# Attention and a softplus layer on one core: the last queries' shift copied on ACT instead of DVE, and one low part moved to GpSimd

## The chip, the cores and the metric

The kernel runs on one core of a Trainium2 chip. The metric is the device time of one execution in microseconds; lower is better. The time of a kernel is the median of its runs, and one more execution is profiled. TensorE (PE, with its weight loads PEld), VectorE (DVE), ScalarE (ACT), GpSimd (POOL) and SyncE (SP, here only a DMA queue) each run their own list of instructions in order, and wait for one another by semaphores.

## The reference, cut to what matters

Rotary attention over 4 batches of 8 heads, 576 positions of 64 numbers, and a layer of 2304 tokens, 512 to 2048 to 512 wide, with softplus between:

```python
q_rot, k_rot = rotate(q), rotate(k)
scores = q_rot @ k_rot.T / sqrt(64)
attn = exp(scores - max(scores))
attn = attn / (sum(attn) + 1e-9)
x = (attn @ v)          # 2304 tokens of 512
h = x @ w_in
g = max(h, 0) + log1p(exp(-abs(h)))
out = g @ w_out
```

All is float32. The kernel splits every operand in a rounded high part and the low part that is left, and adds three products of parts (high times high, low times high, high times low).

## The kernel before, in words

**Stages.** Attention comes first (to about 342 us of the trace), the layer after it. The heads go two at a time: 16 pairs, each in 9 slots, so 144 slots in all. A pair's 64-wide heads stand on partitions 0 to 63 and 64 to 127, so most products are two matmuls of 64 rows.

**What a slot does.** In slot `s` the first pass `p1(s)` (L448, L455) multiplies queries by keys and DVE takes the row maxima (L457). Ten slots later the second pass `p2` (L503) computes the same scores with keys on the partitions, into one of two buffers of PSUM (tile `sp`, pool `ps_2`), and adds the shift (minus the maximum of each query) by two more matmuls of ones with `sm`, which holds the shift as a row. Then `exps` does two exponentials on ACT: L508 writes the rounded one, `ph`; L511 writes the full one back over `sp`. DVE subtracts (L517, `low`) and gives `pl`. Three slots later `pv_half` (L553) multiplies `ph` and `pl` by the values.

**The shift.** POOL splits the maxima into `sh` (L353, L356, `shift1`). `shift2` turns them from columns into rows by small matmuls with an identity (L475), into the unused columns of the very `sp` buffer that `p2` fills next. Queries come in 4 chunks of 128 and a last one of 64. The chunks go in two groups: group 0 (chunks 0 to 2) in the slot with `r == 0`, group 1 (chunk 3 and the last 64 queries, one copy for each head) in the slot with `r == 4`, where `r` is the slot's number within its pair. `shift3` copies the rows to `sm`, on ACT, between the two exponentials of that tile (L484). The last 64 queries alone are copied by DVE, by two instructions of 64x64 at the end of `shift2` (L479), ahead of the second pass of that tile in the program. The tile after it (`r == 4` of its pair, last keys and all queries) is the first to need group 1, in its last two matmuls, those with `onesd`.

**The ropes.** POOL rotates the pairs ahead of time: multiplies with the tables, adds, rounds (`hl` are queries, `kk` keys; part 1 of each is the low part). Pairs 0 and 1 are split between engines to start sooner; pair 1 is `rope_second`, a generator whose steps the table `ROPES` deals out to the first slots. Its last step is the low part of the queries, on DVE. The first pass of pair 1 (slot 9) needs it in its third matmul. `split_v` rounds the values of a pair on ACT and subtracts on POOL (tile `vs`); a dictionary by slot says how many of its steps a slot takes for pair 0.

**What sets the order.** Instructions that go through `pin` stand on their engine in the order in which the program is written; the DMAs of the loop are chained likewise. Nearly all of the work here is pinned, so the slots' order of calls is the order on the engines. A matmul that writes a buffer waits for every earlier reader of that buffer that stands ahead of it in the program.

Of the kernel before, what the change touches and what calls it, by code (L numbers as in the profile page):

```python
# [8 lines left out]
F32 = mybir.dt.float32  # L9
# [5 lines left out]
ALU = mybir.AluOpType  # L15
# [5 lines left out]
HS = 288  # L21
# [24 lines left out]
    127: (3, 2), 131: (3, 3), 136: (4, 0), 140: (4, 1)}  # L46
SPLITS = {}
LEAD = 3
ROPES = {0: ((1, 4),), 1: ((1, 1),), 2: ((1, 1),), 7: ((1, 1),), 8: ((1, 1), (2, 1)),
         **{s: ((2, 1),) for s in range(9, 18)}}  # L50
FIRST = {8: 0, 9: 1, 10: 2, 11: 3}


# [1 line left out]
def rope_attention_softplus_moe(  # L55
# [8 lines left out]
    nc = tc.nc  # L64
# [19 lines left out]
    pin = tc.keep_in_program_order  # L84
# [221 lines left out]
    def attention(es, es_r, es_s, tail, window):  # L306
# [18 lines left out]
        sm = [at1.tile([128, 5, 128], F32R, name=f"sm{i}") for i in range(2)]  # L325
# [4 lines left out]
        rows = (slice(0, 64), slice(64, 128))  # L330
# [17 lines left out]
        def rnd(out, in_, e):  # L348
            if e == "A":
                pin(nc.scalar.copy(out=out, in_=in_))  # L350
            else:
                e = nc.vector if e == "V" else nc.gpsimd
                pin(e.tensor_scalar(out=out, in0=in_, scalar1=1.0, scalar2=0.0, op0=ALU.mult, op1=ALU.add))  # L353

        def tt(out, in0, in1, op, e):
            pin((nc.vector if e == "V" else nc.gpsimd).tensor_tensor(out=out, in0=in0, in1=in1, op=op))  # L356

        def new_hl(p, i):
            if i:
                hl_t[p, i] = kk[p % 3]  # L360
            else:
                hl_t[p, i] = hl_p.tile([128, 2, S], F32R, tag="hl", name="hl")
            return hl_t[p, i]

        def rope_second():
            (qb, qa), (kb, ka) = [[raw_t[1, i][:, j] for j in range(2)] for i in range(2)]
            q, k = new_hl(1, 0), new_hl(1, 1)
            yield tt(ka, ka, tab[:, 0, :], ALU.mult, "P")
            yield tt(kb, kb, tab[:, 1, :], ALU.mult, "P")
            tt(ka, ka, kb, ALU.add, "P")  # L370
            yield rnd(k[:, 0], ka, "A")
            yield tt(qa, qa, tab[:, 0, :], ALU.mult, "P")
            yield tt(k[:, 1], ka, k[:, 0].bitcast(F32), ALU.subtract, "P")
            yield tt(qb, qb, tab[:, 1, :], ALU.mult, "P")
            tt(qa, qa, qb, ALU.add, "V")
            yield rnd(q[:, 0], qa, "A")
            yield tt(q[:, 1], qa, q[:, 0].bitcast(F32), ALU.subtract, "V")

        def rope_steps(p, e="P"):
            for i in (1, 0):  # L380
# [31 lines left out]
        def load_v(p):  # L412
            chain(nc.sync.dma_start(out=vf[p % 2], in_=v[2 * p:2 * p + 2].rearrange("h p c d -> p h c d")))
# [58 lines left out]
        def shift2(p, g, t):  # L472
            for n, c in enumerate((3, 4) if g else range(3)):
                for i, o in enumerate(rows):
                    pin(nc.tensor.matmul(out=t[:, i, HS + n * 64:HS + n * 64 + 64], lhsT=sh[p % 2][o, c, :],  # L475
                                         rhs=identr[o, o], start=True, stop=True))
            if g:
                for i, o in enumerate(rows):
                    pin(nc.vector.tensor_copy(out=sm[p % 2][o, 4, :64], in_=t[o, i, HS + 64:HS + 128]))  # L479
            return t[:, :, HS:HS + (64 if g else 192)]  # L480

        def shift3(p, g, x):
            cs = slice(3, 4) if g else slice(0, 3)
            pin(nc.scalar.copy(out=sm[p % 2][:, cs, :].rearrange("p c (t x) -> p t c x", t=2),  # L484
                               in_=x.rearrange("p t (c x) -> p t c x", x=64)))

        def tile2(n):
            ps2[n] = ps_2.tile([128, 2, 512], F32, tag="s2", name="sp2")
# [70 lines left out]
        def evac(w):  # L559
            p, j = divmod(w, 2)  # L560
            pv = pv_t.pop(w)
            xt = xt_p.tile([D + 1, 2, HS], F32, tag="xt", name="xt")
            if w >= 2 * NP - 3:
                pin(nc.vector.tensor_copy(out=xt, in_=pv[0:D + 1, :, :HS]))
            else:
                pin(nc.scalar.copy(out=xt, in_=pv[0:D + 1, :, :HS]))
            if w > 2 * NP - 3:
                store(w, xt, free)
            else:
                done.append((w, xt))  # L570
# [71 lines left out]
        def first(s):  # L642
            n = FIRST[s]
            tile2(n)
            p2(n)
            exps(n)

        for s in range(NSLOT + LAG + PVD + 1):
            n2, n3 = s - LAG, s - LAG - PVD
            p, r = divmod(s, PER)  # L650
            has2, has3 = 0 <= n2 < NSLOT, 0 <= n3 < NSLOT
            m = n3 % PER
            for n, part in halves[0].get(n3, ()):
                pv_half(n, part)
            if n3 > 0 and m == 0 or has3 and m == 4:
                evac(2 * (n3 // PER) - (m == 0))
            if s > LAG + 3 and has2:
                tile2(n2)
                g = {0: 0, 4: 1}.get(r) if s <= NSLOT + 4 else None
                x = None if g is None else shift2(p - 1, g, ps2[n2])  # L660
                p2(n2)
                if r == 5 and s < NSLOT:
                    p1(s)
                exps(n2, None if g is None else (lambda: shift3(p - 1, g, x)))
            elif s == LAG - 1:
                first(s)
            elif s == LAG + 3:
                shift3(0, 1, shift2(0, 1, ps_2.tile([128, 2, 512], F32, tag="s2", name="st")))
            for n, part in halves[1].get(n3, ()):
                pv_half(n, part)  # L670
            if s < NSLOT and (r != 5 or not p):
                p1(s)
                if r in (6 - (p == 0), 8):
                    shift0(p, r // 8)
            if s == 0:
                wp = ps_2.tile([128, 2, 512], F32, tag="s2", name="wp")
            if s == LAG - 1:
                wp = ps_v.tile([128, 2, 512], F32, tag="pv", name="wp")
            if s < LAG + PVD - 1 and s != LAG - 2:
                for i, o in enumerate(2 * rows):  # L680
                    pin(nc.tensor.matmul(out=wp[:, i % 2, :HS], lhsT=ones[o, :], rhs=hl_t[0, 0][o, 0, :HS], start=True,
                                         stop=True))
            if s == LAG - 3:
                shift3(0, 0, shift2(0, 0, ps_2.tile([128, 2, 512], F32, tag="s2", name="st")))
            if s != LAG - 1 and s in FIRST:
                first(s)
            for n, part in halves[2].get(n3, ()):
                pv_half(n, part)
            if s in FIRST or s > LAG + 3 and has2:
                low(FIRST.get(s, n2))  # L690
            if s == 6:
                shift1(0, 0)
            if r == 7 and PER < s < NSLOT:
                shift1(p, 0)
            if r == 0 and 0 < s <= NSLOT:
                shift1(p - 1, 1)
            if s < NSLOT:
                for x, z in ROPES.get(s, ()):
                    for _ in range(z):
                        next(ropes[x], None)  # L700
                if r == 7 and 2 < p + 2 < NP:
                    ropes[p + 2] = rope_steps(p + 2)
                x = (s + 2) // PER + 1
                if 2 < x < NP:
                    for _ in range(1 + (r == 5)):
                        next(ropes[x], None)
                if r in (3, 5) and 2 < p + 2 < NP:
                    load(p + 2, int(r == 3), chain)
                if r == 6 and p + 1 < NP:
                    load_v(p + 1)  # L710
                if p and r == 6:
                    sv = split_v(p)
                if p and r == 1:
                    corner(p, 0, chain)
                if s == 4 or p and r == 8:
                    corner(p, 1, chain)
            for _ in range({6: 2, 7: 1, 8: 1}.get(s, int(s > 10 and r in (1, 6, 7, 8)))):
                next(sv, None)
            if done and m in (1, 5):
                store(*done.pop(), chain)  # L720
            if n3 % (PER * NH // 2) == 4 and n3 > 4:
                load_sums(n3 // (PER * NH // 2) - 1, chain)
            if n3 % (PER * NH // 2) == 7 and n3 > 7:
                guard(n3 // (PER * NH // 2) - 1)
            if n3 % (PER * NH // 2) == 9 and n3 > 9:
                recip(n3 // (PER * NH // 2) - 1)
            tail(s)
            window(s)
# [151 lines left out]
```

## Time and profile before

| | before |
|---|---|
| median of 3 runs | 749.22 us (748.53 to 750.93) |
| profiled execution | 749.25 us, span of its core 747.5 us |
| PE busy | 709.2 us (95%) |
| DVE busy | 468.9 us (63%) |
| ACT busy | 374.1 us (50%) |
| POOL busy | 310.6 us (42%) |

The span is what the trace covers; 1.75 us of the profiled execution lie around it. Shares over the span mix two stages: in the layer PE alone is busy nearly all the time, in attention four engines are. The timeline gives for each row its start and duration in us, the engine, the line, what is written from what, and in brackets how long the engine sat idle before it and whose end it waited for.

### The profile page before, as it was taken

How to read it: one execution, taken by the hardware profiler on the slowest of the kernel's cores; microseconds unless marked ns; L12 is line 12 of the kernel's file. 1: busy time of each engine (PE TensorE's matmuls, PEld its weight loads, DVE VectorE, ACT ScalarE, POOL GpSimd, SP SyncE). 2: the span in 40 equal slices, each digit the busy share in tenths (PEclk: the TensorE clock that was granted, in tenths of full speed). 3: DMA queues.
4: the chain of work that ended last, by engine and by line, in shares of the span. 5: the costliest groups of instructions: out<-in, count | busy, mean ns of one | idle time of the engine just before them, and what ended most of it. 6: DMA issues, size and time to landing. Idle time of an engine off the chain costs nothing.

```text
span 747.5 us, 15218 instructions
## 1 busy us (share of the span) xinstructions
PE 709.2 (95%) x6075; PEld 656.7 (88%) x6075; DVE 468.9 (63%) x823; ACT 374.1 (50%) x704; POOL 310.6 (42%) x367
## 2 busy tenths in 40 slices
PE   8699998989898999989999999999999999999997
PEld 8688898888888899988989898999999998989896
DVE  6577777777777777756888878454453443344433
ACT  2367777776777676665665654232222222222222
POOL 7768888888888889683000000271310000000000
PEclk9799999999999999999999999999999999999999
DMA  7324343334354453201342322061010010001001
GB/s 253 124 87 129 104 118 94 105 101 123 114 140 140 143 145 96 61 17 52 136 141 91 136 89 89 16 196 43 22 44 0 1 43 0 1 1 43 0 1 43
DMA packets 40151, 61.31 MB, mean 82 GB/s; under 512 B 14288, under 2 KB 26896, under 8 KB 40080
## 3 DMA queue, kind: packets, MB, share of 16 engines
q1 hardware_dynamic: 37200, 55.16, 24.4%
q10 hardware_dynamic: 2880, 5.18, 1.8%
q8 instruction: 48, 0.79, 0.4%
q14 instruction: 23, 0.19, 0.1%
HBM read 48.64 MB, written 7.23 MB: 75 GB/s over the span
## 4 chain that ended last, share of the span: by engine, by line
PE 55%; DVE 0%; ACT 0%; issue 0%
PE hp L234 27%; PE oa L273 13%; PE ob L273 13%; PE pv L553 1%; PE sp L503 1%; DVE wt L292 0%; ACT wt L294 0%; DVE sm L479 0%
## 5 line engine op out<-in xcount | busy, mean ns | idle before, releaser
L234 PE MATMUL hp<-x,wh 128*128 128x384 f32 x768 | 196.3, 336 | 0.0
L246 ACT ACTIVATE e<-e 128x384 f32<-128x384 f32 x96 | 50.5, 526 | 209.7 <-DVE e L244 203.3
L457 DVE TENSOR_REDUCE mx<-sp 128x2 f32<-128x576 f32 x144 | 108.8, 758 | 66.0 <-PE sp L448 53.9
L234 PEld LDWEIGHTS hp<-x,wh 128*128 128x128 f32 x768 | 140.7, 188 | 8.4 <-issue 0.2
L508 ACT ACTIVATE ph<-sp 128x576 fp32r<-128x576 f32 x144 | 93.8, 652 | 93.2 <-PE sp L503 92.5
L234 PE MATMUL hp<-x,wl 128*128 128x384 f32 x384 | 129.3, 337 | 0.0
L553 PE MATMUL pv<-ph,vs 64*128 64x288 f32 (+1 forms) x1152 | 126.7, 298 | 0.4
L517 DVE TENSOR_TENSOR pl<-sp,ph 128x576 fp32r<-128x576 f32 x144 | 108.1, 751 | 19.8 <-ACT sp L511 19.0
L244 DVE TENSOR_SCALAR e<-hp 128x384 int32<-128x384 int32 x96 | 53.4, 556 | 81.5 <-PE hp L234 80.2
L273 PE MATMUL oa<-wh,g 128*128 128x512 f32 x288 | 97.7, 393 | 0.0
L273 PE MATMUL ob<-wh,g 128*128 128x512 f32 x290 | 97.4, 391 | 0.0
L503 PE MATMUL sp<-hl,kk 64*128 64x288 f32 x768 | 76.4, 302 | 20.7 <-DVE sm L479 20.3
L511 ACT ACTIVATE sp<-sp 128x576 f32<-128x576 f32 x144 | 92.7, 644 | 1.0
L356 POOL TENSOR_TENSOR raw<-raw,tab 128x576 f32<-128x576 f32 x60 | 85.9, 1443 | 4.2 <-DMA raw<-qk 4.0
L448 PE MATMUL sp<-kk,hl 64*128 64x288 f32 x768 | 76.3, 300 | 11.8 <-DVE wc L139 5.8
L553 PE MATMUL pv<-pl,vs 64*128 64x288 f32 x576 | 87.2, 292 | 0.0
L249 DVE SCALAR_TENSOR_TENSOR m<-hp,e 128x384 f32<-128x384 f32 x96 | 53.5, 557 | 51.1 <-ACT e L246 51.1
L553 PEld LDWEIGHTS pv<-ph,vs 64*128 64x128 f32 (+1 forms) x1152 | 78.3, 158 | 4.9 <-issue 2.5
L254 DVE TENSOR_TENSOR g<-m,g 128x384 fp32r<-128x384 f32 x96 | 55.2, 575 | 41.8 <-ACT g L251 41.8
L503 PEld LDWEIGHTS sp<-hl,kk 64*128 64x128 f32 x768 | 58.8, 187 | 23.0 <-DVE sm L479 21.9
L448 PEld LDWEIGHTS sp<-kk,hl 64*128 64x128 f32 x768 | 59.7, 187 | 16.4 <-PE pv L553 8.3
L234 PEld LDWEIGHTS hp<-x,wl 128*128 128x128 f32 x384 | 72.0, 188 | 0.0
(112 smaller groups left out, 1039.9 us busy)
## 6 DMA issues: line engine op xcount, KB each, us to landing
raw<-qk SPq DMA_DIRECT2D x29, 576.0 KB
wraw<-w SPq DMA_DIRECT2D x23, 512.0 KB
vf<-v SPq DMA_DIRECT2D x16, 320.0 KB
wraw<-w SPq DMA_DIRECT2D x14, 256.0 KB
x<-xt SPq DMA_DIRECT2D x32, 72.0 KB
xd<-xt SPq DMA_DIRECT2D x32, 72.0 KB
x<-rd SPq DMA_DIRECT2D x16, 144.0 KB
out<-wc ACTq DMA_DIRECT2D x9, 256.0 KB
```

Source lines behind the costliest of these rows:

```text
L234: pin(nc.tensor.matmul(out=hp, lhsT=a[f][:, c * 128:(c + 1) * 128], rhs=piece(j, c)[:, b, :], start=(i == 0), stop=(i == 11),))
L249: pin(nc.vector.scalar_tensor_tensor(out=m, in0=hp, scalar=0.0, in1=e, op0=ALU.max, op1=ALU.add))
L254: pin(nc.vector.tensor_tensor(out=g[:, 1, :], in0=m, in1=g[:, 0, :].bitcast(F32), op=ALU.subtract))
L273: pin(nc.tensor.matmul(out=po[:, z], lhsT=g[:, s, t * 128:(t + 1) * 128], rhs=b[f][:, 512 + z.start:512 + z.stop], start=(first and i == 0 ...
L356: pin((nc.vector if e == "V" else nc.gpsimd).tensor_tensor(out=out, in0=in0, in1=in1, op=op))
L448: pin(nc.tensor.matmul(out=sp[:, i, :HS], lhsT=q[o, a, c * 128:c * 128 + 128], rhs=k[o, b, j * HS:(j + 1) * HS], start=(t == 0), stop=(t = ...
L457: pin(nc.vector.tensor_reduce(out=to, in_=sp[:, :, :HS], axis=AX.X, op=ALU.max, negate=True))
L503: pin(nc.tensor.matmul(out=sp[:, i, :HS], lhsT=lhs, rhs=rhs, start=(t == 0), stop=(t == 3)))
L508: pin(nc.scalar.activation(out=ph, in_=sp, func=AF.Exp, scale=D ** -0.5))
L511: pin(nc.scalar.activation(out=sp, in_=sp, func=AF.Exp, scale=D ** -0.5))
L517: pin(nc.vector.tensor_tensor(out=pl, in0=sp[:, :, :HS], in1=ph.bitcast(F32), op=ALU.subtract))
L553: two.append(pin(nc.tensor.matmul(out=pv[:k, i, :HS], lhsT=lhs, rhs=x[o, j if c is None else i, :], start=first, stop=last)))
```

## The change

Three edits. The two 64x64 copies of the last queries' shift leave DVE and `shift2`, and come behind the other copy of group 1 in `shift3`, on ACT, between the two exponentials. The low part of pair 1's queries goes from DVE to POOL, in slot 8 as before. The splitting of pair 0's values starts in slot 5 instead of 6, with its POOL steps in slots 6 and 7, and the first step of pair 2's rope moves from slot 8 to 9.

```diff
-ROPES = {0: ((1, 4),), 1: ((1, 1),), 2: ((1, 1),), 7: ((1, 1),), 8: ((1, 1), (2, 1)),
-         **{s: ((2, 1),) for s in range(9, 18)}}
+ROPES = {0: ((1, 4),), 1: ((1, 1),), 2: ((1, 1),), 7: ((1, 1),), 8: ((1, 1),), 9: ((2, 2),),
+         **{s: ((2, 1),) for s in range(10, 18)}}
...
-            yield tt(q[:, 1], qa, q[:, 0].bitcast(F32), ALU.subtract, "V")
+            yield tt(q[:, 1], qa, q[:, 0].bitcast(F32), ALU.subtract, "P")
...
-            if g:
-                for i, o in enumerate(rows):
-                    pin(nc.vector.tensor_copy(out=sm[p % 2][o, 4, :64], in_=t[o, i, HS + 64:HS + 128]))
-            return t[:, :, HS:HS + (64 if g else 192)]
+            return t[:, :, HS:HS + (128 if g else 192)]
+
+        def shift3(p, g, x):
+            cs = slice(3, 4) if g else slice(0, 3)
+            w = 64 if g else 192
+            pin(nc.scalar.copy(out=sm[p % 2][:, cs, :].rearrange("p c (t x) -> p t c x", t=2),
+                               in_=x[:, :, :w].rearrange("p t (c x) -> p t c x", x=64)))
+            if g:
+                for i, o in enumerate(rows):
+                    pin(nc.scalar.copy(out=sm[p % 2][o, 4, :64], in_=x[o, i, 64:]))
...
-            for _ in range({6: 2, 7: 1, 8: 1}.get(s, int(s > 10 and r in (1, 6, 7, 8)))):
+            for _ in range({5: 2, 6: 1, 7: 1}.get(s, int(s > 10 and r in (1, 6, 7, 8)))):
```

On PE, at the first tile that carries group 1 (`sp_922`; `sm_126` is the shift, `sp_941` the first pass of that slot, `sp_959` the next tile of the second pass), before:

```order
L475 MATMUL sp_922<-identr,sh_124 128x64 [waits DVE_49,Pool_49]
L475 MATMUL sp_922<-identr,sh_124 128x64 x3
L503 MATMUL sp_922<-hl,kk_100 128x288 [waits DVE_49]
L503 MATMUL sp_922<-hl,kk_100 128x288 x5
L503 MATMUL sp_922<-sm_126,ones 128x288 x2
L448 MATMUL sp_941<-kk_101,hl 128x288 [waits PE_49]
```

and after:

```order
L475 MATMUL sp_922<-identr,sh_124 128x64 [waits DVE_49,Pool_49]
L475 MATMUL sp_922<-identr,sh_124 128x64 x3
L504 MATMUL sp_922<-hl,kk_100 128x288 x6
L504 MATMUL sp_922<-sm_126,ones 128x288 x2
L448 MATMUL sp_941<-kk_101,hl 128x288 [waits DVE_49]
L448 MATMUL sp_941<-kk_101,hl 128x288 x5
```

The rows stand in the same order; the wait of the second pass for DVE is gone, and the first pass behind it has one for DVE (the maxima that free its buffer).

On ACT at the same tile, before:

```order
L508 ACTIVATE ph<-sp_922 128x576 [waits DVE_49,PE_49]
L484 CAST sm_126<-sp_922 128x128
L511 ACTIVATE sp_922<-sp_922 128x2x288 [waits Activation_49]
L508 ACTIVATE ph<-sp_959 128x576 [waits PE_49]
L511 ACTIVATE sp_959<-sp_959 128x2x288
```

and after:

```order
L509 ACTIVATE ph<-sp_922 128x576 [waits PE_49]
L482 CAST sm_126<-sp_922 128x128
L486 CAST sm_126<-sp_922 64x64 x2
L512 ACTIVATE sp_922<-sp_922 128x2x288 [waits DVE_49,Activation_49]
L509 ACTIVATE ph<-sp_959 128x576 [waits PE_49]
```

The two copies come between the exponentials, ahead of the second one, and leave DVE's list (two copies for each of the 16 pairs of heads, 32 in all).

On POOL near the start (`vs_132` are the values of pair 0, `sh_123` its shift, `raw` the rope of pair 2, `hl` the queries of pair 1), before:

```order
L356 TENSOR_TENSOR vs_132<-vf_130,vs_132 128x5x64 [waits DMAHW1_49,Activation_49]
L356 TENSOR_TENSOR raw<-raw,tab 128x576 [waits DMAHW4_49]
L356 TENSOR_TENSOR vs_132<-vf_130,vs_132 128x5x64 [waits Activation_49]
L356 TENSOR_TENSOR sf<-sf,mask 128x2 [waits DVE_49]
L353 TENSOR_SCALAR sh_123<-sf 128x4 [waits Pool_49]
```

and after:

```order
L356 TENSOR_TENSOR vs_132<-vf_130,vs_132 128x5x64 [waits DMAHW1_49,Activation_49]
L356 TENSOR_TENSOR vs_132<-vf_130,vs_132 128x5x64 [waits Activation_49]
L356 TENSOR_TENSOR hl<-raw,hl 128x576 [waits Activation_49]
L356 TENSOR_TENSOR sf<-sf,mask 128x2 [waits DVE_49]
L353 TENSOR_SCALAR sh_123<-sf 128x4 [waits Pool_49]
```

The queries' low part stands behind both halves of the values; the rope multiply of pair 2 that stood between them comes after the shift's split.

## Rows read from the trace of the kernel before

**Rows 1.** Stages: window; length, busy PE, PEld, DVE, ACT, POOL (instructions); clock; DMA

```profile
94.00:150.00 56.00, 51.87 (x706) 49.96 (x708) 41.72 (x74) 40.74 (x77) 46.49 (x54) 1.00 0.38 108
342.00:747.00 405.00, 401.69 (x2019) 363.62 (x2018) 223.67 (x405) 143.41 (x277) 33.06 (x38) 1.00 0.17 54
```

**Rows 2.** Waits, who for whom: us in total, times, longest

```profile
ACT ph L508 <- PE sp L503: 92.5, 106, 5.9
...
POOL sh L353 <- DVE sf L461: 46.4, 14, 10.7
...
PEld sp L503 <- DVE sm L479: 21.9, 15, 1.6
PE sp L503 <- DVE sm L479: 20.3, 15, 1.4
```

**Rows 3.** Timeline around one wait for the two DVE copies, slot r = 4

```profile
92.83 0.75 DVE L517 TENSOR_TENSOR pl<-sp,ph 128x576 fp32r<-128x576 f32 x1
...
93.49 0.45 DVE L479 CAST sm<-sp 64x64 fp32r<-64x64 f32 x2
...
93.99 0.66 PE L503 MATMUL sp<-hl,kk 64*128 64x288 f32 x6 [1.34 <-DVE sm L479]
...
94.84 0.65 ACT L508 ACTIVATE ph<-sp 128x576 fp32r<-128x576 f32 x1 [1.65 <-PE sp L503]
...
95.23 0.76 DVE L457 TENSOR_REDUCE mx<-sp 128x2 f32<-128x576 f32 x1 [1.29 <-PE sp L448]
...
95.39 0.26 ACT L484 CAST sm<-sp 128x128 fp32r<-128x128 f32 x1
...
95.68 0.64 ACT L511 ACTIVATE sp<-sp 128x576 f32<-128x576 f32 x1
...
96.29 0.32 PEld L503 LDWEIGHTS sp<-sm,onesd 128*128 128x128 f32 x2
...
96.89 0.65 ACT L508 ACTIVATE ph<-sp 128x576 fp32r<-128x576 f32 x1 [0.57 <-PE sp L503]
...
97.68 0.76 DVE L457 TENSOR_REDUCE mx<-sp 128x2 f32<-128x576 f32 x1 [0.58 <-PE sp L455]
```

**Rows 4.** Timeline, the same step for group 0, slot r = 0

```profile
104.84 0.41 PE L475 MATMUL sp<-identr,sh 64*128 64x64 f32 x6
...
105.09 0.65 PE L503 MATMUL sp<-hl,kk 64*128 64x288 f32 x6
```

**Rows 5.** Groups by line and shape: count, busy us, mean ns, idle before

```profile
L484 ACT CAST sm<-sp 128x384 fp32r<-128x384 f32 x15 | 7.1, 473 | 0.0
L479 DVE CAST sm<-sp 64x64 fp32r<-64x64 f32 x30 | 6.5, 217 | 0.2
L484 ACT CAST sm<-sp 128x128 fp32r<-128x128 f32 x15 | 3.9, 259 | 0.0
L356 POOL TENSOR_TENSOR hl<-raw,hl 128x576 fp32r<-128x576 f32 x14 | 20.1, 1436 | 1.1
```

**Rows 6.** Timeline near the start, where pair 1's first pass begins

```profile
19.09 1.94 POOL L356 TENSOR_TENSOR raw<-raw,tab 128x576 f32<-128x576 f32 x1
19.78 0.68 ACT L350 CAST hl<-raw 128x576 fp32r<-128x576 f32 x1 [0.36 <-DMA vf<-v]
20.98 0.86 POOL L356 TENSOR_TENSOR vs<-vf,vs 128x320 fp32r<-128x320 f32 x1
22.56 1.98 DVE L356 TENSOR_TENSOR hl<-raw,hl 128x576 fp32r<-128x576 f32 x1
24.59 0.85 PE L448 MATMUL sp<-kk,hl 64*128 64x288 f32 x4 [3.32 <-DVE hl L356]
```

**Rows 7.** Two-microsecond windows behind that, columns as in rows 1

```profile
28.00:30.00 2.00, 2.00 (x20) 2.00 (x18) 0.18 (x1) 1.13 (x2) 2.00 (x3) 0.50 0.95 366
34.00:36.00 2.00, 2.00 (x17) 1.84 (x16) 0.80 (x2) 0.27 (x1) 0.00 (x0) 0.68 0.00 0
36.00:38.00 2.00, 2.00 (x10) 2.00 (x9) 0.00 (x0) 0.95 (x2) 0.00 (x0) 0.50 0.07 12
```

More of the change, by code (lines that the diff above doesn't have):

```diff
@@ L476, in shift2 @@
                                          rhs=identr[o, o], start=True, stop=True))
+            return t[:, :, HS:HS + (128 if g else 192)]
[4 more added lines that the diff above has]
+                               in_=x[:, :, :w].rearrange("p t (c x) -> p t c x", x=64)))
             if g:
                 for i, o in enumerate(rows):
-                    pin(nc.vector.tensor_copy(out=sm[p % 2][o, 4, :64], in_=t[o, i, HS + 64:HS + 128]))
-            return t[:, :, HS:HS + (64 if g else 192)]
[L482 to L485, printed above, removed]
+                    pin(nc.scalar.copy(out=sm[p % 2][o, 4, :64], in_=x[o, i, 64:]))
         def tile2(n):
```

## The prediction

> **What bounds the kernel now.** The windows by stage come first [rows 1]. In the layer PE is busy 401.7 of 405.0 us, and nothing there is touched. In attention PE is busy 51.9 of 56.0 us, DVE 41.7, ACT 40.7, POOL 46.5, so PE is nearest to its limit but idle for 7% of the time; only that idle time can be won. The list of waits says who is ahead [rows 2]: ACT waits for PE's second pass (92.5 us in 106 waits) and POOL for the maxima of PE's first pass (46.4 us in 14); in the timeline DVE sits for 1.29 and 0.58 us in front of such maxima [rows 3]. All three follow PE and catch up with it, so time that PE loses is time of the kernel. PE's largest loss to another engine has its own row: the second pass waits for the two DVE copies 15 times, 20.3 us in total. The waits are alike: none is over 1.4 us, and the mean is 1.35.
>
> The timeline shows how one arises [rows 3]. The transposes of the shift have ended, and the second pass of the same buffer must not write before DVE has read it. DVE is still in the subtraction that began at 92.83, starts the copies at 93.49 and ends them at 93.94; PE goes on at 93.99, having stood for 1.34 us. It is a wait for a reader of the buffer, not for the data, which the next tile alone needs. The sister step is the control [rows 4]: for group 0 no DVE copy stands in between, and the second pass begins at 105.09, before the last of the transposes that began at 104.84 has ended, with no wait.
>
> **The change part by part: the copies.** With the copies behind the first exponential on ACT, no DVE read stands ahead of the second pass; PE should go on as in [rows 4]. That removes 15 waits, **20.3 us** by the matmul row. I take this end; the weight loads of the same matmuls waited 21.9 us [rows 2], so the most is 1.6 us more.
>
> What is late next? I move everything in [rows 3] that hangs on PE 1.34 us earlier and look at the margins. ACT had been idle for 1.65 us before its exponential at 94.84, so it is free 0.31 us before it is wanted. DVE had been idle for 1.29 before the maximum at 95.23 and sheds 0.45 us of copies, so it has 0.40 left. The first pass behind needs its buffer back: the maximum that frees it ended about when the subtraction at 92.83 started, and the pass would start near 93.3. The subtraction itself ends at 93.58; the next tile takes its buffer, and that tile's six score matmuls (0.66 us for six at 93.99) stand ahead of its last weight loads at 96.29, so it starts near 95.5, moved to 94.2. Nothing comes late; the tightest margin is 0.3 us.
>
> What do the copies cost on ACT? No row shows a 64x64 copy there. From above it is 0.26, the wider 128x128 form [rows 5]; along the line through the 473 and 259 ns forms (0.84 ns per element) it is 0.21, and DVE's own copy of that size takes 0.217. I take 0.21 and keep 0.26 as the bound. Put into [rows 3]: the 128x128 copy ends at 95.65, the two new ones at 96.07 (96.17 at the bound). Who waits for them is PE, in the two `onesd` matmuls of the next tile, whose weights loaded at 96.29 without waiting; the cover is 0.22 us (0.12). Behind those matmuls on PE stand the first pass of the next slot and the value products. If the cover were gone, each further 0.1 us would cost 1.5 us in all. The second exponential moves from 95.68 to about 96.1 (96.2) and ends at 96.74 (96.84); the next exponential on ACT starts at 96.89 and waited 0.57 for PE, so it isn't moved; the subtraction behind it on DVE ends before the maximum of 97.68, in front of which DVE sat for 0.58. So I cost the copies on ACT at nothing, between 0 and some 4 us.
>
> One rule speaks against the change. The Trainium skill, page "ScalarE: Activation LUTs", section "Rules for kernel authors", budgets about 0.3 us for each instruction on ScalarE and 0.83 ns per element; by that a copy would take 0.35 us (an estimate). The 259 ns row is below that budget already, its slope of 0.84 agrees. By the skill's figure the last copy would end at 96.35, 0.06 past the load, and the sum would lose 1 to 2 us.
>
> POOL gets no faster but must follow a shorter slot. Of its 46.4 us of waiting one wait is 10.7, so the other 13 average 2.7 us per pair; 1.34 less leaves 1.4. It stays ahead.
>
> **The start.** The low part of pair 1's queries ran on DVE at 22.56 for 1.98 us, behind a subtraction; PE, idle for 3.32 us, went on at 24.59 [rows 6]. On POOL it stands behind the second half of the values and needs ACT's rounded part, which ends at 20.46. The values ran at 20.98 only because a rope multiply of 1.94 us stood in front; without it both halves are done by about 19.09 + 0.86 = 20.0. So the low part starts near 20.5 and takes 1.44 [rows 5], or 1.98 as on DVE: PE goes on at 22.0 (22.5), and wins **2.6 us** (2.1). A loss here would need the part to be 4 us late on POOL, where nothing else is queued in front. The rope of pair 2 moves back by one low part; its POOL work then still ends far ahead of the 10.7 us that POOL waits in front of the next maxima [rows 2], so that costs nothing.
>
> The granted clock adds to it. Behind the idle stretch of 3.32 us the clock is at 0.50, the 1.2 GHz level, in 28 to 30 us, and again in 36 to 38, with 0.68 in 34 to 36 [rows 7]. PE is busy throughout 34 to 38: at 2.4 GHz the same work takes 2 x 0.68 + 2 x 0.50 = 2.4 of those 4.0 us, so 1.6 us could be won there and up to 1.0 in 28 to 30, 0 to 2.6 together. Idle stretches of 1.34 us between dense work left the clock at 1.00 [rows 1], and the one here should shrink to about 0.7, so I take 1.6 of the 2.6. Start: 2.6 + 1.6 = **4.2 us**, between 2.1 and 5.2. It is the least sure term.
>
> **The sum.** 20.3 + 4.2 = 24.5 us. The profiled execution took 749.25 us with a span of 747.5, the median is 749.22, so they agree: 749.25 - 24.5 = **724.7 us**, span 723.0.
>
> **The rivals.**
> 1. The copies come late on ACT. For it: the cover is only 0.12 to 0.22 us. Priced by ACT's dearest copy row, 473 ns, two end at 96.60, 0.31 past the load: 15 x 0.31 = 4.7, so 729.4. The Trainium skill's budget ("ScalarE: Activation LUTs", "Rules for kernel authors") would give a milder form of this, near 726. Against: the 259 ns row is wider than the new copy. Chance 0.14.
> 2. The start gives only its low end: the clock falls as before and the part takes 1.98 on POOL. 749.25 - 20.3 - 2.1 = 726.9. For it: the maxima and exponentials there still follow one another tile by tile, so PE keeps some gaps. Chance 0.17.
> 3. POOL becomes the bound in some pairs. For it: only 14 of 16 pairs show a wait, so two have no reserve; if these two give their 1.34 us back and others a little, 3 to 4 us are lost: 728.2. Against: 1.4 us are left per pair on average. Chance 0.07.
> 4. The wait stays, because something else reads that buffer ahead of the second pass. Then only the start is won: 745.1. Against: the order on PE shows no wait there any more. Chance 0.03.
> 5. Slower: ACT becomes the bound at this step. From 24.5 / 15 = 1.63 us of lateness per pair it eats the whole gain: the copies would have to end at 97.9, 1.1 us each. At 1.3 us each it is 2.0 us per pair, 30 us, hence 754.9. Against: no copy row of ACT is over 0.48. Chance 0.02.
>
> **How the numbers follow.** The forecast has 0.57. Rivals 1 to 3 keep most of the gain and lie between 726 and 730. The lower edge takes both upper ends, 20.3 + 1.6 + 5.2 = 27.1: 722.1. The upper edge takes in rivals 1 to 3 and some addition of two of them: 730.5. Outside 0.3% (2.2 us, about what a measurement of this kernel can tell from no change) on the fast side lie all but rival 5 and mishaps that nothing here shows: faster 0.95, the same 0.02, slower 0.03.
>
> **What would show it right or wrong.** Right: no wait of the second pass for DVE; ACT's idle time before its second-pass exponentials smaller by about 20 us; POOL's waits for the maxima about half; three copies between the exponentials of slot r = 4 with 64x64 copies near 0.2 us; the start of the layer near 317 instead of 342 us [rows 1]. Wrong: a row of PE's `onesd` weight loads waiting for ACT (rival 1); a clock of 0.5 in the windows from 24 to 36 (rival 2); POOL rows in front of which PE waits (rival 3). The time would also be wrong if a removed wait came back at another matmul, for instance at the first pass that waits for DVE's maximum, where I found only some 0.3 us of room.

## The result and the profile after

| | before | changed |
|---|---|---|
| median | 748.88 us (748.42 to 750.93, 4 runs) | 721.14 us (720.26 to 721.95, 4 runs) |
| ratio | 1 | 0.9624, interval 0.9601 to 0.9648 |
| profiled execution | 749.25 us, span 747.5 | 721.84 us, span 720.1 |

The change gained 27.7 us; 24.5 were forecast. The time lies 1.0 us below the lower edge of the range (722.1), so the forecast has the right sign and mechanism and one term that was too small. This section finds which.

The engines of the changed kernel, from the first part of its page:

```profile
PE 703.7 (98%) x6075; PEld 652.5 (91%) x6075; DVE 461.1 (64%) x790; ACT 378.7 (53%) x736; POOL 311.8 (43%) x368
```

The two stages, in windows with the columns of [rows 1]:

```profile
94.00:150.00 56.00, 54.49 (x756) 52.78 (x753) 44.87 (x75) 45.38 (x92) 50.97 (x57) 1.00 0.41 121
315.00:720.00 405.00, 401.32 (x2018) 363.27 (x2016) 223.27 (x405) 143.29 (x277) 34.00 (x39) 1.00 0.17 54
```

In 56 us of attention PE's idle time fell from 4.1 to 1.5 us. The layer takes 405 us as before, with PE busy 401.3 instead of 401.7, so all of the gain lies ahead of it.

The waits that answer to [rows 2], same columns:

```profile
ACT ph L509 <- PE sp L504: 59.2, 90, 3.3
POOL sh L353 <- DVE sf L461: 20.3, 14, 5.0
PE sp L448 <- DVE wc L139: 5.8, 12, 0.5
```

No matmul of the second pass waits for the shift any more (`PE sp <- DVE sm` has no row), and PE's longest list of waits for another engine is now the 5.8 us at first passes behind a weight conversion on DVE, which the kernel before had too. No wait came back elsewhere.

**Where the 27.4 us went.** Two rows cut the time into start, attention and layer: the first pass of slot 15, just behind the start, and the first matmul of the layer (tile `hp`). Before:

```profile
41.15 0.66 PE L448 MATMUL sp<-kk,hl 64*128 64x288 f32 x6 [0.47 <-DVE wc L139]
...
341.79 0.62 PE L234 MATMUL hp<-x,wh 128*128 128x384 f32 x2
```

Changed:

```profile
36.81 0.66 PE L448 MATMUL sp<-kk,hl 64*128 64x288 f32 x6 [0.45 <-DVE wc L139]
...
314.43 0.62 PE L234 MATMUL hp<-x,wh 128*128 128x384 f32 x2
```

The start gave 41.15 - 36.81 = 4.34 us, against a forecast of 4.2. Between the two rows lie 300.64 us before and 277.62 now: 23.02 us, where the forecast had 20.3. With 15 removed waits that is 1.53 us for each, and not the 1.35 that the matmul row had shown.

**Why a wait costs more than its row.** The timeline of PE before shows, ahead of the wait in [rows 3], the transposes:

```profile
92.34 0.31 PE L475 MATMUL sp<-identr,sh 64*128 64x64 f32 x4
```

The same step in the changed kernel, with what follows on the other engines:

```profile
84.94 0.31 PE L475 MATMUL sp<-identr,sh 64*128 64x64 f32 x4
...
85.08 0.64 PE L504 MATMUL sp<-hl,kk 64*128 64x288 f32 x6
...
85.89 0.65 ACT L509 ACTIVATE ph<-sp 128x576 fp32r<-128x576 f32 x1
...
86.44 0.26 ACT L482 CAST sm<-sp 128x128 fp32r<-128x128 f32 x1
...
86.59 0.43 ACT L486 CAST sm<-sp 64x64 fp32r<-64x64 f32 x2
...
87.05 0.64 ACT L512 ACTIVATE sp<-sp 128x576 f32<-128x576 f32 x1
87.34 0.32 PEld L504 LDWEIGHTS sp<-sm,onesd 128*128 128x128 f32 x2
...
87.72 0.76 DVE L518 TENSOR_TENSOR pl<-sp,ph 128x576 fp32r<-128x576 f32 x1 [0.66 <-ACT sp L512]
...
88.72 0.76 DVE L457 TENSOR_REDUCE mx<-sp 128x2 f32<-128x576 f32 x1 [0.25 <-PE sp L455]
```

Before, PE's idle time of 1.34 us ran from the end of the transposes, 92.34 + 0.31 = 92.65, to 93.99. Now the second pass starts 0.14 us after the transposes have started, while the last of them is still in flight. What the wait had cost is therefore 93.99 - (92.34 + 0.14) = 1.51 us: the idle time of the row, and 0.17 us in which two groups of matmuls could have overlapped. 15 x 1.51 = 22.7 of the 23.0 us; taken from the timeline wait by wait, the same distance adds up to 22.8 us. The rest of 0.02 per wait is of the size by which six score matmuls differ in length (0.66 us behind the wait, 0.64 now).

The copies on ACT, as groups by shape:

```profile
L486 ACT CAST sm<-sp 64x64 fp32r<-64x64 f32 x30 | 6.3, 210 | 0.2
L482 ACT CAST sm<-sp 128x128 fp32r<-128x128 f32 x15 | 3.9, 258 | 0.0
```

They end at 87.02. The row of the two `onesd` weight loads begins 0.32 us later, at 87.34, but only the second of the two needs them. The first is for queries 0 to 287, whose shift lies in chunks 0 to 2, so in group 0. By the durations (0.32 for both loads, 0.19 for a single one in a run below) the second begins near 87.47, so the cover is about 0.45 us (an estimate).

### The profile page after: what moved, and what is told of

It reads as the page before. It is cut to its first block, busy times and chain, and to the rows that moved or that the text cites. A ratio compares the mean times of both kernels' runs of the same rounds, so it can differ in the third digit from the quotient of the medians.

```text
span 720.1 us, 15186 instructions
## 1 busy us (share of the span) xinstructions
PE 703.7 (98%) x6075; PEld 652.5 (91%) x6075; DVE 461.1 (64%) x790; ACT 378.7 (53%) x736; POOL 311.8 (43%) x368
## 3 DMA queue, kind: packets, MB, share of 16 engines
q1 hardware_dynamic: 37200, 55.16, 25.4%
## 4 chain that ended last, share of the span: by engine, by line
PE 90%; DVE 4%; ACT 2%; issue 2%; DMA 1%; SPq 0%; DVEq 0%
PE hp L234 28%; PE oa L273 14%; PE ob L273 14%; PE pv L554 13%; PE sp L504 11%; PE sp L448 8%; PE sp L455 1%; DVE mx L457 1%; DVE sp L135 1%; DVE wc L139 1%; PE sp L475 1%; DMA raw<-qk 1%; ACT sp L512 1%; ACT ph L509 1%; DVE pl L518 0%
## 5 line engine op out<-in xcount | busy, mean ns | idle before, releaser
L251 ACT CAST g<-m 128x384 fp32r<-128x384 f32 x96 | 49.1, 511 | 45.0 <-DVE m L249 45.0
```

## The experiments

The medians and ratios are each taken against runs of the kernel before beside them. The table cuts each kernel's profiled execution at the same two rows, slot 15's first pass and the first `hp` matmul. What lies between holds the 15 waits and nothing of the start. Where copies are repeated they write the same values again, so nothing is left out of any kernel.

| kernel | median us | ratio to before, interval | slot 15 | layer | between |
|---|---|---|---|---|---|
| before | 748.88 | | 41.15 | 341.79 | 300.64 |
| changed | 721.14 | 0.9624 (0.9601 to 0.9648) | 36.81 | 314.43 | 277.62 |
| before, copies moved alone | 726.31 | 0.9688 (0.9666 to 0.9709) | 41.50 | 319.19 | 277.69 |
| before, start edits alone | 744.63 | 0.9927 (0.9900 to 0.9953) | 36.73 | 337.38 | 300.65 |
| before, low part on GpSimd alone | 743.49 | 0.9920 (0.9892 to 0.9947) | 36.59 | 337.33 | 300.74 |
| before, splitting and rope alone | 748.51 | 0.9984 (0.9970 to 0.9998) | 39.93 | 340.57 | 300.64 |
| before, DVE copies twice | 763.13 | 1.0177 (1.0149 to 1.0206) | 38.96 | 353.36 | 314.40 |
| changed, ACT copies ahead of the second pass | 737.55 | 0.9838 (0.9814 to 0.9862) | 36.92 | 330.93 | 294.01 |
| changed, the late copies on DVE | 726.14 | 0.9712 (0.9683 to 0.9740) | 35.01 | 318.24 | 283.23 |
| changed, ACT copies twice | 725.15 | 0.9694 (0.9671 to 0.9716) | 36.95 | 317.77 | 280.82 |
| changed, ACT copies four times | 738.96 | 0.9871 (0.9846 to 0.9896) | 36.88 | 331.65 | 294.77 |
| changed, fillers at the start | 720.51 | 0.9629 (0.9607 to 0.9651) | 35.41 | 313.08 | 277.67 |

The theory under test (A): a removed wait gives its idle time and the overlap of some 0.2 us. The rival (B): it gives its idle time alone, and the remaining gain came from the start or from the clock. Of the clock the kernel before already says something: between the two rows it never falls.

```profile
42.00:341.00 299.00, 272.64 (x3712) 261.40 (x3708) 219.46 (x379) 215.67 (x401) 249.69 (x288) 1.00 0.37 108
```

**The copies alone.** The kernel before with the copies moved, start untouched.

```diff
-            if g:
-                for i, o in enumerate(rows):
-                    pin(nc.vector.tensor_copy(out=sm[p % 2][o, 4, :64], in_=t[o, i, HS + 64:HS + 128]))
...
+            if g:
+                for i, o in enumerate(rows):
+                    pin(nc.scalar.copy(out=sm[p % 2][o, 4, :64], in_=x[o, i, 64:]))
```

> Only the two 64x64 shift copies go to ACT; the start stays as in the kernel before. Theory A (what a wait costs is more than its idle row, since without it the second pass begins before the last transposes have ended: 1.54 us per wait, 15 waits, 23.1 us): 726 us. Theory B (a wait costs its idle row, 1.35 us each, 20.3 us, and the rest of the gain belongs to the start): 729 us.

It took 726.31 us. Between the two rows lie 277.69 us, 22.95 less than before and the same as in the changed kernel, while slot 15 stands at 41.50, as late as before. The size of the copies' gain doesn't come from the start or from a clock that the start improves: theory A.

**The start alone.** The kernel before with the other edits (`ROPES` as in the change).

```diff
...
-            yield tt(q[:, 1], qa, q[:, 0].bitcast(F32), ALU.subtract, "V")
+            yield tt(q[:, 1], qa, q[:, 0].bitcast(F32), ALU.subtract, "P")
...
-            for _ in range({6: 2, 7: 1, 8: 1}.get(s, int(s > 10 and r in (1, 6, 7, 8)))):
+            for _ in range({5: 2, 6: 1, 7: 1}.get(s, int(s > 10 and r in (1, 6, 7, 8)))):
```

> Only the start is changed (low part of pair 1's queries on POOL, values split two slots sooner, pair 2's rope one slot later); the copies stay on DVE. Theory A: the start gives 4.3 us, so 744.7 us, and the 15 waits stand at 20.3 us as before. Theory B: the start gives what is left of 28 us, 7 to 8 us, so about 741 us.

744.63 us. Its 15 waits stay (20.2 us in the matmul row), and what lies between the two rows is 300.65, as before. Its gain is 4.42 us at slot 15 and 5.2 us by the medians beside it (before took 749.84 us there). The copies alone gained 23.5 us beside the same runs; 23.5 + 5.2 = 28.7, against 27.7 for both: the parts add, within what the intervals allow.

**The wait made longer.** Each DVE copy of the kernel before is done twice.

```diff
-                for i, o in enumerate(rows):
+                for i, o in 2 * tuple(enumerate(rows)):
                     pin(nc.vector.tensor_copy(out=sm[p % 2][o, 4, :64], in_=t[o, i, HS + 64:HS + 128]))
```

> The kernel before with each of the two DVE copies issued twice (four copies of 64x64, the same values written again), so each wait grows by two copies, 0.43 us, and nothing else is changed. Theory A and B alike: idle of the second pass for DVE 15 x 1.78 = 26.7 us, time up by 15 x 0.43 = 6.5 us to 755.5 us. Rival (part of a wait is absorbed by engines that catch up in it): up by less than 4 us.

A miss: 763.13 us, 13.3 more than before where 6.5 were expected. The wait row, the windows and PE at one such wait:

```profile
PE sp L503 <- DVE sm L479: 28.1, 15, 2.0
```

```profile
68.00:72.00 4.00, 3.21 (x51) 3.09 (x48) 3.41 (x6) 3.03 (x5) 3.91 (x5) 1.00 0.87 298
72.00:76.00 4.00, 2.93 (x21) 2.64 (x22) 1.77 (x7) 1.45 (x3) 3.83 (x4) 0.64 0.44 115
```

```profile
73.07 1.04 PE L503 MATMUL sp<-hl,kk 64*128 64x288 f32 x6 [1.87 <-DVE sm L479]
```

The idle time grew by 7.8 us, 0.52 for each wait. The stretch between the two rows grew by 13.76. The other 6 us go with the granted clock: behind this wait of 1.87 us it is 0.64, and six score matmuls take 1.04 instead of 0.66 us. In the kernel before, where the wait in the same place is 1.34 us, the window reads 1.00:

```profile
72.00:76.00 4.00, 2.66 (x38) 2.38 (x35) 2.39 (x6) 2.32 (x6) 3.97 (x3) 1.00 0.46 158
```

The clock fell like that behind four of the 15 waits, those at 73, 217, 298 and 339 us: in the windows 74 to 76, 217 to 219, 299 to 301 and 340 to 342 us it reads 0.50, the 1.2 GHz level. Behind two others of the same length (53 to 55, 95 to 97) it reads 1.00; what sets the four apart stays open. So this kernel can't tell A from B, but it shows a second loss that a wait longer by half a microsecond can bring.

**A shorter wait in the same place.** The changed kernel, with the ACT copies ahead of the second pass, where the DVE copies had been.

```diff
             return t[:, :, HS:HS + (128 if g else 192)]
...
+            if g:
+                for i, o in enumerate(rows):
+                    pin(nc.scalar.copy(out=sm[p % 2][o, 4, :64], in_=t[o, i, HS + 64:HS + 128]))
...
-            if g:
-                for i, o in enumerate(rows):
-                    pin(nc.scalar.copy(out=sm[p % 2][o, 4, :64], in_=x[o, i, 64:]))
```

> The changed kernel, but the two ACT copies stand ahead of the second pass, where DVE's stood. ACT does an evacuation of 0.64 us there first, so the second pass should wait for ACT about 0.9 to 1.0 us in each of 15 slots. Theory A (idle plus about 0.2 us that a wait costs on top): 15 x 1.15 = 17 us over the changed kernel, 738 us. Theory B (idle alone): 15 x 0.95 = 14 us, 735 us. If the engine alone mattered and not the place: 721 us.

737.55 us, as A has it. One of the waits in the timeline:

```profile
87.30 0.31 PE L475 MATMUL sp<-identr,sh 64*128 64x64 f32 x4
...
88.04 0.43 ACT L479 CAST sm<-sp 64x64 fp32r<-64x64 f32 x2
...
88.52 0.67 PE L504 MATMUL sp<-hl,kk 64*128 64x288 f32 x6 [0.91 <-ACT sm L479]
```

The waits sum to 13.3 us by the matmul row, 0.89 each; the stretch grew by 294.01 - 277.62 = 16.39 us, 1.09 each. From the transposes' start plus 0.14 to the second pass are 88.52 - 87.44 = 1.08 us (15.9 us over all 15). The same 0.2 us over the row, at a wait two thirds as long: B is out. It also shows that ACT alone doesn't bring the gain.

**The place kept, the engine put back.** The changed kernel, with the two copies in their new place but on DVE.

```diff
-                    pin(nc.scalar.copy(out=sm[p % 2][o, 4, :64], in_=x[o, i, 64:]))
+                    pin(nc.vector.tensor_copy(out=sm[p % 2][o, 4, :64], in_=x[o, i, 64:]))
```

> The changed kernel, but the two copies stay on DVE while standing where ACT's stand (behind the second pass, between the exponentials). Theory A (the place ahead of the second pass is what cost, not the engine): the second pass has no wait for DVE and the time stays near the changed kernel's, 721 us; DVE may hold up the maximum behind it by up to 0.5 us per pair, so 721 to 728. Rival (taking 0.45 us per pair from DVE is what helped): 15 x 0.45 = 7 us or more are lost even without such a wait, with DVE ahead of PE nowhere.

726.14 us, inside the 721 to 728 expected. The second pass doesn't wait, but the timeline shows a new chain:

```profile
85.67 0.46 DVE L486 CAST sm<-sp 64x64 fp32r<-64x64 f32 x2 [0.57 <-ACT sm L482]
...
86.16 0.76 DVE L457 TENSOR_REDUCE mx<-sp 128x2 f32<-128x576 f32 x1
86.22 0.64 ACT L512 ACTIVATE sp<-sp 128x576 f32<-128x576 f32 x1 [0.58 <-DVE sm L486]
...
86.97 0.81 PEld L455 LDWEIGHTS sp<-kk,qd 128*128 128x128 f32 x6 [0.37 <-DVE mx L457]
```

DVE waits 0.57 us for ACT's copy, its own copies hold up the maximum behind them, and the next first pass needs that maximum's buffer back; ACT's second exponential waits 0.58 us in turn. The waits of that first pass have a row of their own, which the changed kernel lacks:

```profile
PEld sp L455 <- DVE mx L457: 5.2, 14, 0.4
```

The stretch is 283.23 us, 5.6 more than with the copies on ACT. With the place changed first, the place (behind the second pass) thus gives 17.4 of the 23.0 us and the engine the other 5.6. Counted in the other order, by the kernel with ACT's copies ahead of the second pass, the engine alone gives 300.64 - 294.01 = 6.6 and the place 16.4.

**ACT's margin.** The changed kernel, with the ACT copies done twice, and four times.

```diff
-                for i, o in enumerate(rows):
+                for i, o in 2 * tuple(enumerate(rows)):
                     pin(nc.scalar.copy(out=sm[p % 2][o, 4, :64], in_=x[o, i, 64:]))
```

> The changed kernel with each of the two ACT copies issued twice (the same values again), so the last one ends some 0.45 to 0.5 us later. In the changed kernel's trace the last copy ends at 87.02 and the weights that need it load at 87.34, a cover of 0.32 us. Theory (cover of 0.3 us): 0.1 to 0.2 us late in each of 15 slots plus up to 0.2 us for the wait itself, 723 to 727 us. Rival (ACT was already the bound at this step): 15 x 0.5 us or more, 729 us or over.

> The same with each copy issued four times: the last one ends 1.3 to 1.5 us later than in the changed kernel, 1.0 to 1.2 us past the load. Theory: 15 x (1.0 to 1.4) us over the changed kernel, 736 to 742 us, and the weight loads of the matmuls with onesd wait for ACT. Rival (the slots behind take the delay up): under 730 us.

Twice: 725.15 us, and the stretch is 3.2 us longer, 0.21 for each added pair of copies of 0.48 us. So over half of such a pair lies under cover. Its timeline:

```profile
87.12 0.91 ACT L486 CAST sm<-sp 64x64 fp32r<-64x64 f32 x4
...
87.87 0.39 PEld L504 LDWEIGHTS sp<-sm,onesd 128*128 128x128 f32 x2
...
88.06 0.64 ACT L512 ACTIVATE sp<-sp 128x576 f32<-128x576 f32 x1
...
88.72 0.76 DVE L518 TENSOR_TENSOR pl<-sp,ph 128x576 fp32r<-128x576 f32 x1 [1.14 <-ACT sp L512]
```

The row of the two `onesd` loads starts at 87.87, before the copies end at 88.03, and is only 0.07 us longer (0.39 against 0.32). The groups of the `onesd` matmuls, in the changed kernel and here:

```profile
L504 PE MATMUL sp<-sm,onesd 128*128 128x288 f32 x32 | 7.1, 303 | 0.0
L504 PE MATMUL sp<-sm,onesd 128*128 128x288 f32 x32 | 8.0, 329 | 0.2 <-ACT sm L486 0.2
```

That is 0.9 us of busy time and 0.2 of waiting more, 1.1 in all. What moved by the full length of the copies is the second exponential, and behind it DVE's subtraction (it waits 1.14 instead of 0.66 us); the weight conversion behind that on DVE comes late, and its row with PE grows from 5.8 to 7.8 us. The two paths together account for 3.1 of the 3.2 us. Four times: 738.96 us, and now the second of the two `onesd` loads waits for ACT with its matmul, the first doesn't:

```profile
PE sp L504 <- ACT sm L486: 11.0, 15, 1.1
```

```profile
89.65 0.19 PEld L504 LDWEIGHTS sp<-sm,onesd 128*128 128x128 f32 x1
...
90.79 0.19 PEld L504 LDWEIGHTS sp<-sm,onesd 128*128 128x128 f32 x1 [0.95 <-ACT sm L486]
```

From twice to four times the copies grow by 0.92 us (1.83 against 0.91) and the stretch by 294.77 - 280.82 = 13.95 us, 0.93 for each of 15: once the cover is gone, the whole length counts.

**The parts of the start.** The kernel before with the low part on GpSimd alone, and with the earlier splitting and the later rope alone (`ROPES` as in the change).

```diff
-            yield tt(q[:, 1], qa, q[:, 0].bitcast(F32), ALU.subtract, "V")
+            yield tt(q[:, 1], qa, q[:, 0].bitcast(F32), ALU.subtract, "P")
```

> Kernel before with one edit alone: the low part of pair 1's queries on GpSimd; ropes and the splitting of the values as before. Theory A (the place of the low part is the whole gain of the start; the splitting only makes room on GpSimd): the low part is wanted on GpSimd at 20.5, right when ACT's rounded part ends, ahead of the rope multiply that stood at 19.09, and PE's first pass of pair 1 goes on near 22.3 instead of 24.59, as with all start edits together; the rope and the second half of the values move back by 2.8 us. About 744.6 to 746 us. Theory B (both edits are needed): the values' second half and the shift's second group, now some 3 us later on GpSimd, hold up PE or ACT a few slots on, and the time is 747 to 749 us with a new row of PE or ACT waiting for GpSimd near 25 to 32 us.

```diff
...
-            for _ in range({6: 2, 7: 1, 8: 1}.get(s, int(s > 10 and r in (1, 6, 7, 8)))):
+            for _ in range({5: 2, 6: 1, 7: 1}.get(s, int(s > 10 and r in (1, 6, 7, 8)))):
```

> Kernel before with the other start edit alone: values split two... slots sooner and pair 2's rope a slot later; the low part stays on DVE. Theory A: PE's first pass of pair 1 waits for DVE's low part as before. At most 1 us is won, if DVE's low part, no longer beside a 1.94 us rope multiply on GpSimd, takes 0.75 instead of 1.98 us: 748 to 749 us. Theory B: the low part was slow only because GpSimd ran beside it, and without that PE goes on 1.2 us sooner and the clock recovers: 745.5 to 747 us.

The low part alone: 743.49 us, all of what both edits give (744.63) and 1.1 us less than the 744.6 to 746 of theory A. GpSimd starts it, without the other edit, when ACT's rounded part is there:

```profile
20.65 1.41 POOL L356 TENSOR_TENSOR hl<-raw,hl 128x576 fp32r<-128x576 f32 x1 [1.40 <-ACT hl L350]
...
22.11 0.54 PE L448 MATMUL sp<-kk,hl 64*128 64x288 f32 x4 [0.72 <-POOL hl L356]
```

The rope and the values that stand behind it on GpSimd come later and nobody misses them: no PE wait for them appears, and slot 15 stands at 36.59. The splitting alone: 748.51 us, 1.1 less than before beside it. PE still waits for DVE's low part, which now takes 1.15 us (0.75 expected) instead of the 1.98 of [rows 6]:

```profile
23.14 1.15 DVE L356 TENSOR_TENSOR hl<-raw,hl 128x576 fp32r<-128x576 f32 x1
...
24.34 0.53 PE L448 MATMUL sp<-kk,hl 64*128 64x288 f32 x4 [2.48 <-DVE hl L356]
```

In the whole change the splitting is thus not needed for the gain.

**The clock at the start.** The changed kernel with 16 more of the filler matmuls that the kernel already has (into a buffer that nobody reads), in three gaps of the start.

```diff
             elif s == LAG + 3:
                 shift3(0, 1, shift2(0, 1, ps_2.tile([128, 2, 512], F32, tag="s2", name="st")))
+                for _ in range(1):
+                    for i, o in enumerate(2 * rows):
+                        pin(nc.tensor.matmul(out=wp[:, i % 2, :HS], lhsT=ones[o, :], rhs=hl_t[0, 0][o, 0, :HS], start=True, stop=True))
...
+            if s == LAG - 1 or s == LAG + 1:
+                for _ in range(1 + (s == LAG + 1)):
+                    for i, o in enumerate(2 * rows):
+                        pin(nc.tensor.matmul(out=wp[:, i % 2, :HS], lhsT=ones[o, :], rhs=hl_t[0, 0][o, 0, :HS], start=True, stop=True))
```

> The changed kernel with 16 filler matmuls on PE in three gaps of the start (after the first passes of slots 9, 11 and ahead of that of slot 13), each filling being shorter than its gap. Theory (the clock falls because PE stands idle for about half the time from 26 to 30 us; this costs 1.6 us): the granted clock stays at 1.00 from 28 to 36 us and the time is 719.5 to 720.5 in every run, against 720.3 or 721.9 for the changed kernel. Rival (the fillers delay the chain of maxima, or the clock falls in any case): 721.5 to 723 us.

The changed kernel's windows at the start, columns as in [rows 7]:

```profile
28.00:30.00 2.00, 1.29 (x18) 1.17 (x20) 1.34 (x2) 0.57 (x3) 1.96 (x2) 1.00 0.65 245
30.00:32.00 2.00, 2.00 (x15) 1.83 (x12) 0.76 (x1) 0.00 (x0) 2.00 (x2) 0.62 0.00 0
32.00:34.00 2.00, 2.00 (x11) 1.72 (x10) 0.00 (x0) 1.37 (x3) 1.60 (x2) 0.52 0.10 16
34.00:36.00 2.00, 2.00 (x31) 2.00 (x32) 1.90 (x4) 0.83 (x3) 0.00 (x0) 1.00 0.10 16
```

With the fillers:

```profile
28.00:30.00 2.00, 1.61 (x20) 1.39 (x22) 1.42 (x2) 0.59 (x4) 1.92 (x3) 1.00 0.84 321
30.00:32.00 2.00, 2.00 (x21) 1.84 (x18) 0.76 (x1) 0.13 (x1) 2.00 (x2) 1.00 0.01 2
32.00:34.00 2.00, 2.00 (x27) 1.83 (x26) 1.33 (x2) 1.73 (x4) 1.82 (x2) 1.00 0.19 33
```

The clock stays at 2.4 GHz and slot 15 comes 1.40 us sooner. The median is 720.51 us (720.19 to 720.67), against 720.26 to 721.95 for the changed kernel: two of its four runs, with a mean clock of 0.999 and 1.000, already reach this time (720.45 and 720.26), with the fillers all four do, though two of them lie just above the 720.5 expected. By the intervals the two medians can't be told apart. That the fillers make it steady isn't shown by four runs: the kernel with the late copies on DVE has none of the 16, and three of its four runs read 1.000 too.

## Why the prediction was right and wrong

**The 15 waits: mechanism right, term too small.** The step that failed is "**20.3 us** by the matmul row. I take this end", with "the most is 1.6 us more". The 15 waits gave 23.0 us, above both. An idle row runs from the end of the matmul ahead to the start of the one that waited; without the wait the second pass starts before that end. [rows 4] had shown this, as the prediction itself says ("before the last of the transposes that began at 104.84 has ended"), but it was read only as "no wait" and not as a price: 0.25 us after a group of 0.41, so 0.16 us of overlap, and 15 x 0.16 = 2.4 us more. With it the term is 22.7 and the sum 26.9, hence 722.4 us. The copies alone (22.95 us with the start untouched) and the shorter wait of the fourth experiment (0.89 by its row, 1.09 in time) settle that it is this and not the start or the clock. By the medians 27.7 - 23.0 = 4.7 us are left for the start, inside its bounds of 2.1 to 5.2.

**The copies on ACT at nothing: right.** They took 210 ns, as worked out, and no matmul waits for them, so rival 1 fell. The deadline was read too early: the prediction (and the description ahead of it) has both `onesd` matmuls need the copies, but only the second does. The cover is about 0.45 us and not the 0.32 to the first load (0.22 forecast). The Trainium skill, page "ScalarE: Activation LUTs", section "Rules for kernel authors", budgets about 0.3 us for an ACTIVATE and 0.83 ns per element; by that the prediction put such a copy at 0.35 us (an estimate). The measured 0.21 decides. The trace calls these copies CAST, but its ACTIVATE of 576 elements is below the budget too, with 0.65 us against 0.78 (an estimate).

**What is late next: nothing, but one path was not priced.** Its "the tightest margin is 0.3 us" stands well beside the 0.25 us that DVE has left in front of the maximum at 88.72. But the prediction priced the `onesd` loads alone ("each further 0.1 us would cost 1.5 us in all"). Copies done twice showed a second way, which took the larger part of the loss (2.0 of 3.2 us): second exponential, subtraction, weight conversion, first pass. The price itself was right: past the cover, from twice to four times, 0.1 us cost 1.5 us.

**The start: right in sum, in part by luck, wrong in one part.** PE went on at 22.29, 2.30 us sooner (2.6 forecast, bounds 2.1 to 2.6), and slot 15 came 4.34 us sooner, so 2.04 us came behind it (1.6 forecast): 0.3 too much and 0.4 too little. The 0.3 lies ahead of the low part: PE came to the first two matmuls of that pass at 21.27 instead of 20.98 us. With the copies alone and with the DVE copies twice, where the start is that of the kernel before, it came at 21.36 and 21.27, so this is how executions differ. The clock did fall again, to 0.62 and 0.52 in two windows, the sign that was named for rival 2; but it fell later and for a shorter time than in [rows 7], so the sum held all the same. The prediction gave the earlier splitting a part in it ("The values ran at 20.98 only because a rope multiply of 1.94 us stood in front"); the low part moved alone gave as much.

**POOL and ACT.** POOL's waits for the maxima went from 46.4 to 20.3 us; without the longest the 13 others average 1.18 us, against 1.4 forecast from 2.7. POOL stayed ahead (rival 3 fell), and the drop of 1.57 us per pair again speaks for 1.5 us per wait. ACT's idle time before its second-pass exponentials fell by 33 us where "about 20" was forecast; nothing in the sum hung on it. Rival 5's 754.9 should read 754.75 (749.25 - 24.5 + 30). The layer starts at 314.4, not near 317. Rivals 4 and 5 showed no sign.

## What to carry to other kernels

Price a wait of TensorE by where the waiting matmul would have started, not by its idle row: look for the same step without a wait in the same trace and take the distance from start to start. Where a buffer's next writer waits for a small reader, move the reader behind the write of something else before choosing its engine: here the place gave 16.4 to 17.4 us and the engine 5.6 to 6.6, by the order in which they are counted. When two edits come together, one alone on the chip tells which is needed; here the low part alone gave all that both gave at the start.

## What the runs showed of the hardware

A wait of TensorE between dense matmuls cost 0.2 us more than its idle row: 1.53 against 1.35 us, and 1.09 against 0.89 us.

Waits of 1.87 us between dense stretches were followed by a lower granted clock at 4 of 15 places (0.50 in the windows behind them, six matmuls in 1.04 instead of 0.66 us), the 15 waits of about 1.35 us in the kernel before at none. That cost about 6 us beside the 7.8 us of idle time.

The start isn't the same in each execution: in three kernels whose programs differ up to slot 15 only in pair 0's two copies, behind 32 us (before, copies alone, DVE copies twice), its first pass came at 41.15, 41.50 and 38.96 us, and the third is ahead in the clock before those copies: four matmuls took 0.53 us at 24.88, against 0.85 at 24.59 in the kernel before. A part of the 4.34 us of the start can be that spread; the medians put the start at 5.2 and 6.1 us. The time follows the mean clock of a run: beside the experiments the kernel before took 745.94 to 747.19 us in five runs at 0.998 and 749.81 to 751.27 in ten at 0.991. The changed kernel's run at 0.998 took 721.84 us, 24.1 to 25.4 less than those five; with 23.0 us for the waits, 1.1 to 2.4 us of the start's gain are left at the same clock, and the rest goes with the clock.

One subtraction of the same shape took DVE 1.98 us in the kernel before and 1.15 us with the splitting moved, GpSimd's work on a rope running beside it both times; the subtraction of `pl`, one of whose inputs is in PSUM, took 0.76 us beside the same work. In the kernel before and with the splitting moved, the GpSimd multiply that was running when DVE began:

```profile
22.53 1.40 POOL L356 TENSOR_TENSOR raw<-raw,tab 128x576 f32<-128x576 f32 x1
```

```profile
22.27 1.40 POOL L356 TENSOR_TENSOR raw<-raw,tab 128x576 f32<-128x576 f32 x1
```

It ends at 23.93 and 23.67 us, and DVE ends 0.6 us behind it in both: at 22.56 + 1.98 = 24.54 and at 23.14 + 1.15 = 24.29. So the two durations differ by how much of that multiply was still to run. The Trainium skill, page "GPSIMD Engine Reference", section "1. Specifications", names contention of the two engines over the SBUF interfaces that they share, among others with VectorE instructions that have two inputs in SBUF. The rows agree: of these two subtractions only the one with both inputs in SBUF was held up.
